# Set one's weight splits shared between GpSimd and VectorE, and set two's first token pieces nine slots later

## The chip, the cores and the metric

The kernel runs on one core of one Trainium2 chip. The metric is the device time of one execution in microseconds (us); lower is better. TensorE multiplies matrices, ScalarE, VectorE and GpSimd do the elementwise work, and SyncE issues the DMA transfers.

## What is computed

The reference, cut to what matters:

```python
def _moe_ref(x, w_gate, w1, w2):            # x: (2304, 512), from a chunked attention
    P = exp(x @ w_gate - max)               # then 8 rounds of row and column scaling
    out = 0
    for e in range(8):
        h = np.maximum(x @ w1[e], 0.0)      # (2304, 1024)
        out += P[:, e:e + 1] * (h @ w2[e])
    return out

def _moe2_ref(x, w_in, w_out):              # d_ff 2048
    h = x @ w_in
    return (h * np.clip(h + 3.0, 0.0, 6.0) / 6.0) @ w_out
```

Everything is float32. The kernel keeps float32 accuracy by splitting every operand into a rounded high part and the remainder (low part), and by doing three matmuls for one.

## The kernel before

After a first stretch (attention, gate, expert 0, up to about 277 us) the 2304 tokens are worked in three sets of 768. In each set the 28 quarter-experts of experts 1 to 7 are 28 **steps**; the loop is `for s in slots`. A step is seven **slots**, and in each slot TensorE does one of seven products of the first layer (a seven-product scheme for 2x2 blocks, six matmuls of 384 columns each, line 937) and, in set one, one of six token tiles of the second layer of the step before (`mm2_chunk`, six matmuls of 512 columns, line 1077). The products of a step share three PSUM banks called `ha`, `hb`, `hc`, drawn from a pool of two: the order of the products is a, b, a, b, c, b, c, and the third bank, c, takes the place of a as soon as a has been read.

What a step needs beside TensorE, in set one:

- VectorE adds the products (`first_sums`, line 979: results called `u2`, `u3`, `p1`) and takes the low part of the first hidden block (`h_out`, line 954). ScalarE copies the first product (line 983), applies the ReLU (958) and rounds to the high part (953, 959); GpSimd subtracts to get the low part of three hidden blocks (960). The next step's `mm2_chunk` reads all of these (`H`).
- The weights of the quarter-expert are prepared once, in set one, and stored for the other sets: seven first-layer blocks in tile `W1` (from raw tile `r1`, with three sums by VectorE, lines 831 and 837), and eight second-layer blocks, four in tile `W2` (from raw tile `r2`) and four in tile `SS` (from `s2`, three sums of `r2` by VectorE, lines 848 and 854). A split is a **piece** (`cut_piece`): ScalarE rounds to the high part (858), then GpSimd or VectorE subtracts for the low part (859). A step has four pieces of `W1` (`w1_piece`, the last one half as wide and on VectorE), two of `W2` (`w2_piece`) and two of `SS` (`w2s_piece`), seven of the eight on GpSimd.
- The stores go through SyncE's queue (`w1_keep` line 875, `w2_store` line 896), as do the loads of raw weights (`raw_load` 808, `raw_load2` 821 to 823). The tile `SS` has a pool of one buffer (line 1556), and so has `s2` (1560); `W2` has two.

The order of the side work is set by a planner: `book` (line 1621) puts an operation into the first slot from `g` on in which the engines' load, by a table of costs, stays under its limits; `book_cuts` (1643) does so for pieces; `at_slot` then files it. Within a slot the work for the products is written first and then the side work, each engine takes its own instructions strictly in the order written, and an instruction that has to wait holds all behind it on its engine. In every fourth step (4, 8, ... 24) VectorE also adds six finished expert sums to the result (line 1085). Conversion of the last layer's weights (`cv_op`, lines 202 to 220) is spread over set one and two.

In set two (28 steps from step 28 on) no weights are split; the tokens of set one's result are cut into pieces for the last layer (`x2_cut`, split by ScalarE 694 and GpSimd 695; `x2_keep`, stored by SyncE 1277), booked by `book_x2` from a fixed slot on (line 1767), followed by the last layer's own weights (`book_ahead`).

Of the kernel before, what the change touches and what calls it, by code (L numbers as in the profile page):

```python
# [9 lines left out]
F32 = mybir.dt.float32  # L10
# [18 lines left out]
def chunk_attention_moe_mlp(  # L29
# [23 lines left out]
    nc = tc.nc  # L53
# [799 lines left out]
        o, x, y, op = ((2, t[:, 1], r[:, 0], ALU.add), (3, r[:, 1], t[:, 2], ALU.subtract))[n - 1]  # L853
        nc.vector.tensor_tensor(out=t[:, o], in0=x, in1=y, op=op)

    def cut_piece(hi, lo, r, lo_eng):

        nc.scalar.activation(out=hi, in_=r, func=AF.Copy)  # L858
        lo_eng.tensor_tensor(out=lo, in0=r, in1=hi.bitcast(F32), op=ALU.subtract)  # L859

    def cut_ops(w, r, o0, o1, lo_eng):

        cut_piece(w[:, o0:o1, 0], w[:, o0:o1, 1], r, lo_eng)

    PIECES = ((0, 2), (2, 4), (4, 6), (6, 7))

    def w1_piece(s, z, lo_eng=nc.gpsimd):
        o0, o1 = PIECES[z]
        r = raw1[s.k].rearrange("p o k f -> p o (k f)")[:, o0 + 1:o1 + 1]
        cut_ops(W1t[s.b].rearrange("p o a k f -> p o a (k f)"), r, o0, o1, lo_eng)  # L870
        if z == 3:
            raw1.pop(s.k)

    def w1_keep(s):
# [4 lines left out]

    W2t = {}  # L880

    def w2_piece(s, z, lo_eng=nc.gpsimd):
        if z == 0:
            W2t[s.i] = pools["W2"].tile([128, 4, 2, 256], F32R, tag="W2", name=f"W2_{s.i}")
        cut_ops(W2t[s.i], raw2[s.k][:, 2 * z:2 * z + 2], 2 * z, 2 * z + 2, lo_eng)

    SS = {}

    def w2s_piece(k, z):
        if z == 0:  # L890
            SS[k] = pools["SS"].tile([128, 4, 2, 256], F32R, tag="SS", name=f"SS_{k}")
        cut_ops(SS[k], raw2[k, "s"][:, 2 * z:2 * z + 2], 2 * z, 2 * z + 2, nc.gpsimd)

    def w2_store(k, o, t):
        n = t.shape[1]
# [448 lines left out]
    with tc.manual_schedule():  # L1344
# [221 lines left out]
        def at_slot(i, z, fn, *a):  # L1566
            sides.setdefault((7 * i + z) // 7, {}).setdefault((7 * i + z) % 7, []).append((fn, *a))
# [53 lines left out]
        def book(g, fn, *a, dve=0.0, act=0.0, pool=0.0):  # L1621
            need = (("DVE", dve), ("ACT", act), ("POOL", pool))
            def full(e, c):
                v = load[e]
                if e != "DVE":
                    if g < 7 * TURN + 7:
                        return v[g] + c > CAP[e]
                    return max(sum(v[g - 2:g + 1]), sum(v[g - 1:g + 2]), sum(v[g:g + 3])) + c > 6.05
                old = new = 0.0
                for i in range(max(0, g - 7), g + 8):  # L1630
                    old = max(0.0, old + v[i] - (2.08 if i >= 7 * TURN else 2.23))
                    new = max(0.0, new + v[i] + c * (i == g) - (2.08 if i >= 7 * TURN else 2.23))
                    if new > max(SLACK, old):
                        return True
                return False

            while any(c and full(e, c) for e, c in need):
                g += 1
            use(g, dve, act, pool)
            at_slot(0, g, fn, *a)  # L1640
            return g

        def book_cuts(g, end, pieces):
            for fn, *a in pieces:
                if a[-1] == 3 and fn is w1_piece:
                    g = book(g + 1, fn, *a, nc.vector, act=0.4, dve=0.8)
                else:
                    g = book(g, fn, *a, act=0.62, pool=1.3)
            assert g < end, (g, end, pieces)
            return g  # L1650

        for s in slots[:NEXP]:
            if s.i > 1:
                g = max(7, 7 * (s.i - 2) + 3)
                for n in range(NSUM):
                    g = book(g, w1_sum, s.k, n, dve=1.0 if n == 0 else 0.8)
            if s.i == 1:
                for z in range(4):
                    at_slot(0, z, w1_piece, s, z, nc.vector if z > 1 else nc.gpsimd)
                at_slot(0, 6, w1_keep, s)  # L1660
            elif s.i:
                g = book_cuts(max(g + 1, 7 * (s.i - 1)), 7 * s.i,
                              [(w1_piece, s, z) for z in range(4)])
                at_slot(0, g + 2, w1_keep, s)
            if s.i and s.i + 2 < NEXP:
                at_slot(s.i - 1, 4, raw_load, s.k + 2)
        for s in slots[:TURN]:
            if s.i:
                at_slot(s.i - 1, 0, raw_load2, s.k)
            g = 7 * s.i  # L1670
            if s.i:
                h = book_cuts(g + 1, g + 7, [(w2_piece, s, z) for z in range(2)])
            else:
                h = g + 3
                at_slot(0, g + 1, w2_piece, s, 0)
                at_slot(0, h, w2_piece, s, 1, nc.vector)
            at_slot(0, h + 2, w2_keep, s)
            for n in range(NSUM):
                g = book(g, w2_sum, s.k, n, dve=1.0 if n == 0 else 0.8)
            h = book_cuts(max(g, h) + 1, 7 * s.i + 8,  # L1680
                          [(w2s_piece, s.k, z) for z in range(2)])
            at_slot(0, h + 2, w2s_keep, s.k)

        for s in slots[NEXP:]:
            if s.load:
# [78 lines left out]

        at_slot(ends[0], 6, x2_T, 0, 0)
        at_slot(ends[0], 6, x2_T, 0, 1)
        g = 7 * ends[0] + 9
        for kl in range(2):
            g = book_x2(g, 0, kl, 3)
        g = book_ahead(g + 4, range(NEXP, NEXP + NG4))  # L1770
# [107 lines left out]
```

## Time and profile before

| | us |
|---|---|
| median of 3 runs | 1917.66 (1917.62 to 1919.47) |
| profiled execution | 1915.93 |
| its span, first to last instruction | 1914.2 |
| TensorE busy in the span | 1892.2 (99%) |
| VectorE busy | 1587.4 (83%) |
| GpSimd busy | 1240.1 (65%) |
| ScalarE busy | 813.9 (43%) |

The profiled execution is 1.7 us under the median. TensorE's idle time in the whole span is 22 us, so what the side engines do counts only where TensorE waits for them. Set one's steps run from about 277 us to 731 us.

### The profile page before, as it was taken

The page shows a single profiled execution, that of the slowest core. Times are in us where ns is not written, and L with a number is a line of the kernel's source. Part 1 is how long each engine was busy: PE and PEld are TensorE (multiplying, and loading weights), DVE is VectorE, ACT ScalarE, POOL GpSimd, SP SyncE. Part 2 cuts the span into 40 slices and gives each one's busy share as a digit, 9 for nine tenths or more (in the row PEclk, how much of TensorE's full clock was granted, in tenths as well). Part 3 has the DMA queues.
Part 4 walks back from the last instruction along what each step waited for, and adds up shares of the span by engine and source line. Part 5 has one row for each costly group of instructions (what it writes and reads, how often), then busy time and mean ns, then how long its engine had stood idle before and what let it go on. Part 6 is the DMA issues. An engine that isn't in the chain of part 4 may idle for free.

```text
span 1914.2 us, 34452 instructions
## 1 busy us (share of the span) xinstructions
PE 1892.2 (99%) x11915; PEld 1810.9 (95%) x11915; DVE 1587.4 (83%) x2366; ACT 813.9 (43%) x1632; POOL 1240.1 (65%) x1072
## 2 busy tenths in 40 slices
PE   9999999999999999999999999999999999999998
PEld 8789998988889898999999999999999999999998
DVE  6677577788788858999999989898888888797867
ACT  5333335555555543434343333233333345454452
POOL 3323248888888875768887556576788755566544
PEclk9999999999999999999999999999999999999999
DMA  9987569999999997999999899989999999999984
GB/s 212 225 221 232 207 222 355 329 314 320 316 324 315 326 345 269 365 339 352 359 375 395 292 331 328 314 295 343 343 363 372 387 343 335 339 304 310 291 266 147
DMA packets 353661, 594.18 MB, mean 310 GB/s; under 512 B 56512, under 2 KB 171600, under 8 KB 353360
## 3 DMA queue, kind: packets, MB, share of 16 engines
q1 hardware_dynamic: 353488, 591.98, 90.0%
q8 instruction: 95, 1.56, 0.3%
q14 instruction: 78, 0.64, 0.1%
HBM read 405.68 MB, written 186.20 MB: 309 GB/s over the span
## 4 chain that ended last, share of the span: by engine, by line
PE 85%; DVE 8%; DMA 3%; issue 2%; ACT 1%; POOL 0%; DVEq 0%; SPq 0%; ACTq 0%; POOLq 0%
PE o L1195 18%; PE hb L937 16%; PE ha L937 10%; PE acc L1077 10%; PE hc L937 10%; PE o L1185 9%; PE h L587 5%; PE acc L624 5%; DVE u L979 1%; DMA W2R<-wsc 1%; PE pv_None L439 1%; DVE accM L1220 1%; PE sc_None L351 1%; DVE r L837 1%; DMA wsc<-W 1%
## 5 line engine op out<-in xcount | busy, mean ns | idle before, releaser
L937 PE MATMUL hb<-X,W 128*128 128x384 f32 x1944 | 393.2, 337 | 5.4 <-DVE u L979 5.1
L937 PEld LDWEIGHTS hb<-X,W 128*128 128x128 f32 x1944 | 338.8, 188 | 17.5 <-DVE u L979 11.0
L1195 PE MATMUL o<-Hb,W2R 128*128 128x384 f32 x1296 | 275.5, 334 | 1.8 <-DMA W2R<-wsc 1.3
L937 PE MATMUL hc<-X,W 128*128 128x384 f32 x1296 | 261.1, 336 | 1.5 <-DVE H L954 0.7
L937 PE MATMUL ha<-X,W 128*128 128x384 f32 x1296 | 260.7, 335 | 0.6 <-DVE m L1257 0.6
L1077 PE MATMUL acc<-W,H 128*128 128x512 f32 x1008 | 258.9, 391 | 0.7 <-POOL H L960 0.5
L937 PEld LDWEIGHTS hc<-X,W 128*128 128x128 f32 x1296 | 226.3, 188 | 8.2 <-DVE u L979 2.5
L1195 PEld LDWEIGHTS o<-Hb,W2R 128*128 128x128 f32 x1296 | 229.1, 188 | 2.4 <-issue 1.6
L1220 DVE SCALAR_TENSOR_TENSOR accM<-o,accM 128x768 f32<-128x768 f32 x209 | 198.6, 950 | 39.1 <-PE o L1195 25.0
L937 PEld LDWEIGHTS ha<-X,W 128*128 128x128 f32 x1296 | 226.0, 188 | 3.8 <-DVE m L1257 0.9
L1195 PE MATMUL o<-Ha,W2R 128*128 128x384 f32 x1056 | 227.3, 334 | 1.4 <-ACT accM L1218 1.4
L859 POOL TENSOR_TENSOR Hb<-u,Hb 128x384 fp32r<-128x384 f32 x144 | 164.7, 1146 | 80.2 <-ACT Hb L858 69.7
L1077 PEld LDWEIGHTS acc<-W,H 128*128 128x128 f32 x1008 | 187.4, 188 | 30.2 <-POOL H L960 3.2
L859 POOL TENSOR_TENSOR W<-r,W 128x512 fp32r<-128x512 f32 (+1 forms) x139 | 193.9, 1426 | 15.4 <-ACT W L858 15.2
L1195 PEld LDWEIGHTS o<-Ha,W2R 128*128 128x128 f32 x1056 | 186.8, 188 | 2.0 <-ACT accM L1218 1.7
L859 POOL TENSOR_TENSOR Ha<-t,Ha 128x384 fp32r<-128x384 f32 x89 | 98.6, 1108 | 90.6 <-ACT Ha L858 81.0
L859 POOL TENSOR_TENSOR Hb<-p,Hb 128x384 fp32r<-128x384 f32 x94 | 111.5, 1186 | 66.1 <-ACT Hb L858 45.4
L979 DVE TENSOR_TENSOR u<-hc,u 128x384 f32<-128x384 f32 x216 | 118.4, 548 | 41.2 <-PE hc L937 41.1
L979 DVE TENSOR_TENSOR u<-hb,p 128x384 f32<-128x384 f32 x216 | 118.5, 549 | 32.6 <-PE hb L937 27.0
L859 POOL TENSOR_TENSOR Ha<-u,Ha 128x384 fp32r<-128x384 f32 x96 | 112.5, 1173 | 48.1 <-ACT Ha L858 43.0
L858 ACT ACTIVATE Hb<-u 128x384 fp32r<-128x384 f32 x144 | 75.6, 525 | 157.0 <-DVE u L675 54.2
L1185 PE MATMUL o<-W2R,Hb 128*128 128x256 f32 x837 | 129.0, 281 | 0.0
(201 smaller groups left out, 3587.2 us busy)
## 6 DMA issues: line engine op xcount, KB each, us to landing
W2R<-wsc SPq DMA_DIRECT2D x280, 512.0 KB, 6.0
W<-wsc SPq DMA_DIRECT2D x504, 256.0 KB, 5.8
wsc<-W SPq DMA_DIRECT2D x28, 1792.0 KB, 7.3
wsc<-SS SPq DMA_DIRECT2D x28, 1024.0 KB, 9.1
wsc<-m SPq DMA_DIRECT2D x112, 256.0 KB, 5.9
r<-in_moe_w_dram SPq DMA_DIRECT2D x84, 256.0 KB, 7.9
wsc<-W SPq DMA_DIRECT2D x28, 768.0 KB, 8.5
X<-xsc SPq DMA_DIRECT2D x21, 768.0 KB, 8.1
```

The lines of the kernel that those rows point to most:

```text
L351: nc.tensor.matmul(out=sc[z][64 * par:64 * par + 64, g * CH:(g + 1) * CH], lhsT=qT[64 * z:64 * z + 64, 2 * hp + par, c * CH:(c + 1) * CH], ...
L439: nc.tensor.matmul(out=ps[c][64 * par:64 * par + 64, g * CH:(g + 1) * CH], lhsT=vt[tt][64 * c:64 * c + 64, 2 * hp + par, :], rhs=aT[64 * c ...
L587: nc.tensor.matmul(out=hps[:, :n], lhsT=w[:, a, kk, :], rhs=xx[:, kk, :], start=(kk == 0 and a == 0 and xx is xh), stop=(kk == KD - 1 and ...
L624: nc.tensor.matmul(out=o, lhsT=w[:, a, c] if turned else hx[:, c], rhs=hx[:, :n] if turned else w[:, a, :], start=(f == 0 and hx is hi and ...
L858: nc.scalar.activation(out=hi, in_=r, func=AF.Copy)
L859: lo_eng.tensor_tensor(out=lo, in0=r, in1=hi.bitcast(F32), op=ALU.subtract)
L937: nc.tensor.matmul(out=ps[:, :HN], lhsT=W1t[s.b][:, wo, a, kl, :], rhs=x[:, b, kl, :], start=(start and kl == 0 and a == 0 and b == 0), st ...
L979: nc.vector.tensor_tensor(out=o, in0=ps[b][:, :HN], in1=x, op=ALU.add)
L1077: nc.tensor.matmul(out=o, lhsT=s.Hs[:, fi, hx, t * 128:(t + 1) * 128], rhs=w[:, 0::3, a, :] if fi == 0 else w[:, 1:3, a, :], start=(s.j % ...
L1185: nc.tensor.matmul(out=o[:, t * 256:(t + 1) * 256], lhsT=hs[q][:, b, t * 128:(t + 1) * 128], rhs=w[:, q, a, :], start=(q, a, b) == mm[0] a ...
L1195: nc.tensor.matmul(out=ps[:, d, :HN], lhsT=w[:, q, a, d * 128:(d + 1) * 128], rhs=hs[q][:, b, :], start=(q, a, b) == mm[0] and not again, ...
L1220: nc.vector.scalar_tensor_tensor(out=dst, in0=src, scalar=sc, in1=dst, op0=ALU.mult, op1=ALU.add)
```

## The change

In set one the low parts of two more pieces of a step are taken by VectorE: the second piece of `W2` and the first piece of `SS`. A piece can now be made in two halves (`half=0` is ScalarE's rounding, `half=1` the subtraction), and for the three pieces on VectorE the rounding is booked at least one slot ahead of the subtraction. The sums of `s2` are booked around the first piece of `SS`; a variable `kept2` keeps a step's sums and pieces of `SS` behind the last piece of the step before. The planner's costs of the sums go down from 1.0 and 0.8 to 0.9 and 0.7. In the first step the second piece of `W2` goes to GpSimd and two pieces of `W1` are a slot later. In set two the first token piece is booked from slot 18 of the set on, not 9; all that is booked behind it moves too.

The core of the diff (signatures that only pass `half` and `lo_eng` on are left out):

```diff
+    def cut_piece(hi, lo, r, lo_eng, half=None):
+        if half != 1:
+            nc.scalar.activation(out=hi, in_=r, func=AF.Copy)
+        if half != 0:
+            lo_eng.tensor_tensor(out=lo, in0=r, in1=hi.bitcast(F32), op=ALU.subtract)
...
-    def w2s_piece(k, z):
-        if z == 0:
+    def w2s_piece(k, z, lo_eng=nc.gpsimd, half=None):
+        if half != 1 and k not in SS:
             SS[k] = pools["SS"].tile([128, 4, 2, 256], F32R, tag="SS", name=f"SS_{k}")
...
+        ON_DVE = {w1_piece: 3, w2_piece: 1, w2s_piece: 0}
         def book_cuts(g, end, pieces):
             for fn, *a in pieces:
-                if a[-1] == 3 and fn is w1_piece:
-                    g = book(g + 1, fn, *a, nc.vector, act=0.4, dve=0.8)
+                if a[-1] == ON_DVE[fn]:
+                    w = 0.4 if fn is w1_piece else 0.62
+                    g = book(g + 1, fn, *a, nc.vector, 0, act=w)
+                    g = book(g + 1, fn, *a, nc.vector, 1, dve=w + 0.25)
...
-                    at_slot(0, z, w1_piece, s, z, nc.vector if z > 1 else nc.gpsimd)
+                    at_slot(0, z + z // 2, w1_piece, s, z, nc.vector if z > 1 else nc.gpsimd)
...
-                at_slot(0, h, w2_piece, s, 1, nc.vector)
+                at_slot(0, h, w2_piece, s, 1)
             at_slot(0, h + 2, w2_keep, s)
-            for n in range(NSUM):
-                g = book(g, w2_sum, s.k, n, dve=1.0 if n == 0 else 0.8)
-            h = book_cuts(max(g, h) + 1, 7 * s.i + 8,
-                          [(w2s_piece, s.k, z) for z in range(2)])
+            g = max(g, kept2)
+            g = book(g, w2_sum, s.k, 0, dve=0.9)
+            c = book(g + 1, w2s_piece, s.k, 0, nc.vector, 0, act=0.62)
+            g = book(g + 1, w2_sum, s.k, 1, dve=0.7)
+            c = book(max(c, g) + 1, w2s_piece, s.k, 0, nc.vector, 1, dve=0.87)
+            g = book(g, w2_sum, s.k, 2, dve=0.7)
+            h = book_cuts(g + 1, 7 * s.i + 12, [(w2s_piece, s.k, 1)])
+            h = max(c, h)
             at_slot(0, h + 2, w2s_keep, s.k)
+            kept2 = h + 1
...
-        g = 7 * ends[0] + 9
+        g = 7 * ends[0] + 18
```

What this makes of the instruction order is shown at three places. In the rows below a name's first number is the step (of `W1`: the buffer; of `r1`, the quarter-expert), and the brackets name what the instruction waits for (`DMAHW` is a lane of DMA transfers; `Activation` is ScalarE, `Pool` GpSimd).

**ScalarE in step 5**, the step behind an expert's end, from the rounding of `H_5` on. Before:

```order
L953 ACTIVATE H_5_4470<-ha_5_4463 128x384 [waits PE_49,Pool_49]
L858 ACTIVATE W1_0_3126<-r1_6_4281 128x256
L858 ACTIVATE W2_5_4507<-r2_5_4338 128x2x256 [waits DMAHW3_49,DMAHW2_49]
L858 ACTIVATE SS_5_4547<-s2_5_4477 128x2x256 [waits DMAHW0_49,DVE_49]
L858 ACTIVATE SS_5_4547<-s2_5_4477 128x2x256 [waits DVE_49]
L958 ACTIVATE u3_5_4542<-u3_5_4542 128x384 [waits DVE_49]
L959 ACTIVATE H_5_4470<-u3_5_4542 128x384 [waits Activation_49]
```

Now:

```order
L859 ACTIVATE SS_4_4361<-s2_4_4334 128x2x256 [waits DVE_49]
L955 ACTIVATE H_5_4466<-ha_5_4459 128x384 [waits PE_49,Pool_49]
L859 ACTIVATE W1_0_3126<-r1_6_4278 128x256
L859 ACTIVATE W2_5_4518<-r2_5_4336 128x2x256 [waits DMAHW1_49,DMAHW0_49]
L859 ACTIVATE W2_5_4518<-r2_5_4336 128x2x256 [waits DMAHW3_49,DMAHW2_49]
L859 ACTIVATE SS_5_4543<-s2_5_4521 128x2x256 [waits DMAHW5_49,DVE_49]
L960 ACTIVATE u3_5_4536<-u3_5_4536 128x384 [waits DVE_49]
L961 ACTIVATE H_5_4466<-u3_5_4536 128x384 [waits Activation_49]
```

The second piece of `SS_4`, which stood in step 4, is now rounded in step 5, and `SS_5`, in the same single buffer, is begun in that step too.

**SyncE at the end of step 4 and in step 5**, around the store of `SS_4`. Before:

```order
L896 DMA wsc2_2_100<-W2_4_4360 128x3x512 [waits DMAHW7_49,Pool_49]
L896 DMA wsc2_2_100<-SS_4_4399 128x4x512 [waits DMAHW0_49,Pool_49]
L821 DMA r2_6_4481<-in_moe_w2_dram 128x2x256 [waits DMAHW1_49]
L822 DMA r2_6_4481<-in_moe_w2_dram 128x256 [waits DMAHW2_49]
L823 DMA r2_6_4481<-in_moe_w2_dram 128x256 [waits DMAHW3_49]
```

Now:

```order
L898 DMA wsc2_2_100<-W2_4_4358 128x3x512 [waits DMAHW7_49,DVE_49,Pool_49]
L821 DMA r2_6_4474<-in_moe_w2_dram 128x2x256 [waits DMAHW0_49,DVE_49]
L822 DMA r2_6_4474<-in_moe_w2_dram 128x256 [waits DMAHW1_49]
L823 DMA r2_6_4474<-in_moe_w2_dram 128x256 [waits DMAHW2_49]
L184 DMA cv_8_4478<-in_moe2_w_out_dram 128x1024 [waits DMAHW3_49]
L184 DMA cv_9_4480<-in_moe2_w_out_dram 128x1024 [waits DMAHW4_49]
L898 DMA wsc2_2_100<-SS_4_4361 128x4x512 [waits DMAHW5_49,Pool_49]
```

The store of `SS_4` has moved behind the loads of step 5 (its slot was the sixth of step 4 and is now the fourth of step 5); the first rounding of `SS_5` waits for it on lane 5. The same holds at steps 9, 13, 17, 21 and 25.

**VectorE in step 0**, the last four sums but one of the step. Before:

```order
L979 TENSOR_TENSOR u3_0_3836<-hb_0_3806,p1_0_3794 128x384 [waits PE_49]
L859 TENSOR_TENSOR W1_1_3784<-r1_1_3130,W1_1_3784 128x256 [waits Activation_49]
L859 TENSOR_TENSOR W2_0_3817<-r2_0_3517,W2_0_3817 128x2x256 [waits DMAHW0_49,Activation_49]
L979 TENSOR_TENSOR u3_0_3836<-hc_0_3842,u3_0_3836 128x384 [waits DVE_49,PE_49]
L557 TENSOR_REDUCE scs_3861<-cp7_3859 128x8 [waits PE_49]
```

Now:

```order
L981 TENSOR_TENSOR u3_0_3839<-hb_0_3804,p1_0_3794 128x384 [waits PE_49]
L861 TENSOR_TENSOR W1_1_3784<-r1_1_3130,W1_1_3784 128x2x256 [waits Activation_49]
L981 TENSOR_TENSOR u3_0_3839<-hc_0_3845,u3_0_3839 128x384 [waits DVE_49,PE_49]
L861 TENSOR_TENSOR W1_1_3784<-r1_1_3130,W1_1_3784 128x256 [waits Activation_49]
L557 TENSOR_REDUCE scs_3864<-cp7_3862 128x8 [waits PE_49]
```

The narrow piece of `W1` now stands behind the sum of `u3`, and its rounding on ScalarE stands behind that sum's ReLU and rounding; behind it on VectorE are four small operations of the gate's scaling and the sum `p1`.

## Rows read from the trace of the kernel before

**Rows 1.** The page, busy time of each engine in the span.

```profile
PE 1892.2 (99%) x11915; PEld 1810.9 (95%) x11915; DVE 1587.4 (83%) x2366; ACT 813.9 (43%) x1632; POOL 1240.1 (65%) x1072
```

**Rows 2.** Stretches: length, busy PE, PEld, DVE, ACT, POOL, granted clock, DMA share, GB/s.

```profile
280.00:300.00 20.00, 17.82 (x91) 15.83 (x90) 17.55 (x24) 9.63 (x21) 16.39 (x13) 1.00 0.83 290
300.00:320.00 20.00, 18.59 (x90) 15.92 (x89) 12.38 (x17) 11.12 (x22) 17.21 (x14) 1.00 1.06 385
...
310.00:725.00 415.00, 411.81 (x2048) 369.23 (x2047) 325.65 (x417) 217.96 (x435) 336.26 (x257) 1.00 0.93 324
...
1910.00:1914.20 4.20, 0.00 (x0) 0.00 (x0) 0.83 (x2) 0.00 (x0) 0.00 (x0) 0.80 0.50 170
```

**Rows 3.** Waits (us in total, times, longest): PE's in the span, ACT's in 310:725.

```profile
PE hb L937 <- DVE u L979: 5.1, 10, 1.6
...
ACT SS L858 <- DMA wsc<-SS: 9.8, 6, 4.4
```

**Rows 4.** The tile SS in 310:725, durations in ns min/median/max, and its store's landing.

```profile
L858 ACT ACTIVATE SS<-s x52: 612/621/635, 315.8 to 709.9; 128x512 fp32r<-128x512 f32 x52
L859 POOL TENSOR_TENSOR SS<-s,SS x52: 1277/1476/1765, 316.5 to 711.3; 128x512 fp32r<-128x512 f32 x52
...
DMA to landing us min/median/max: 6.6/9.1/12.7
```

**Rows 5.** Groups of instructions in 310:725: busy us, mean ns of one, idle before.

```profile
L831 DVE TENSOR_TENSOR r<-r 128x512 f32<-128x512 f32 x24 | 29.7, 1239 | 0.0
L859 DVE TENSOR_TENSOR W<-r,W 128x256 fp32r<-128x256 f32 x25 | 28.9, 1157 | 0.0
...
L859 POOL TENSOR_TENSOR W<-r,W 128x512 fp32r<-128x512 f32 x126 | 176.0, 1429 | 0.7 <-ACT W L858 0.5
```

**Rows 6.** Timeline of PE in the step that starts at 415.16: start us, us.

```profile
415.16 1.30 PE L937 MATMUL ha<-X,W 128*128 128x384 f32 x6
416.30 1.54 PE L1077 MATMUL acc<-W,H 128*128 128x512 f32 x6
417.69 1.21 PE L937 MATMUL hb<-X,W 128*128 128x384 f32 x6
...
424.94 1.22 PE L937 MATMUL hc<-X,W 128*128 128x384 f32 x6
...
430.84 1.21 PE L937 MATMUL ha<-X,W 128*128 128x384 f32 x6
```

**Rows 7.** Timelines of ACT and POOL in that step.

```profile
428.89 0.53 ACT L958 ACTIVATE u<-u 128x384 f32<-128x384 f32 x1 [5.12 <-DVE u L979]
...
418.82 7.86 POOL L859 TENSOR_TENSOR W<-r,W 128x512 fp32r<-128x512 f32 x5
...
431.02 1.03 POOL L960 TENSOR_TENSOR H<-p,H 128x384 fp32r<-128x384 f32 x1
```

**Rows 8.** Timelines of PE, DVE, ACT and POOL at set one's start.

```profile
283.95 1.31 PE L937 MATMUL hb<-X,W 128*128 128x384 f32 x6 [1.57 <-DVE u L979]
...
277.56 0.68 DVE L848 TENSOR_TENSOR s<-r 128x512 f32<-128x512 f32 x1
278.28 0.43 DVE L854 TENSOR_TENSOR s<-s,r 128x256 f32<-128x256 f32 x1
...
286.22 0.55 DVE L979 TENSOR_TENSOR p<-hb,p 128x384 f32<-128x384 f32 x1
...
285.33 0.53 ACT L958 ACTIVATE u<-u 128x384 f32<-128x384 f32 x1 [2.52 <-DVE u L979]
...
279.10 3.79 POOL L859 TENSOR_TENSOR W<-r,W 128x512 fp32r<-128x512 f32 x3 [12.79 <-ACT W L858]
```

**Rows 9.** Timelines of PE and ACT at set two's start.

```profile
744.67 0.61 PE L1195 MATMUL o<-Hb,W2R 128*128 128x384 f32 x2 [0.56 <-POOL Hb L859]
...
754.42 0.79 PE L1195 MATMUL o<-Ha,W2R 128*128 128x384 f32 x3 [1.37 <-ACT accM L1218]
...
753.15 0.52 ACT L694 ACTIVATE m<-m 128x384 fp32r<-128x384 f32 x1 [2.26 <-DMA x2sc<-m]
```

More of the change, by code (lines that the diff above doesn't have):

```diff
@@ L854, in w2_sum, with cut_ops, w1_piece @@
         nc.vector.tensor_tensor(out=t[:, o], in0=x, in1=y, op=op)
[L856 to L863, printed above, removed]
+    def cut_piece(hi, lo, r, lo_eng, half=None):
[3 more added lines that the diff above has]
+            lo_eng.tensor_tensor(out=lo, in0=r, in1=hi.bitcast(F32), op=ALU.subtract)
+    def cut_ops(w, r, o0, o1, lo_eng, half=None):
+        cut_piece(w[:, o0:o1, 0], w[:, o0:o1, 1], r, lo_eng, half)
     PIECES = ((0, 2), (2, 4), (4, 6), (6, 7))
-    def w1_piece(s, z, lo_eng=nc.gpsimd):
+    def w1_piece(s, z, lo_eng=nc.gpsimd, half=None):
         o0, o1 = PIECES[z]
         r = raw1[s.k].rearrange("p o k f -> p o (k f)")[:, o0 + 1:o1 + 1]
-        cut_ops(W1t[s.b].rearrange("p o a k f -> p o a (k f)"), r, o0, o1, lo_eng)
-        if z == 3:
+        cut_ops(W1t[s.b].rearrange("p o a k f -> p o a (k f)"), r, o0, o1, lo_eng, half)
+        if z == 3 and half != 0:
             raw1.pop(s.k)
@@ L880, in chunk_attention_moe_mlp, with w2_piece @@
     W2t = {}
-    def w2_piece(s, z, lo_eng=nc.gpsimd):
+    def w2_piece(s, z, lo_eng=nc.gpsimd, half=None):
         if z == 0:
             W2t[s.i] = pools["W2"].tile([128, 4, 2, 256], F32R, tag="W2", name=f"W2_{s.i}")
-        cut_ops(W2t[s.i], raw2[s.k][:, 2 * z:2 * z + 2], 2 * z, 2 * z + 2, lo_eng)
+        cut_ops(W2t[s.i], raw2[s.k][:, 2 * z:2 * z + 2], 2 * z, 2 * z + 2, lo_eng, half)
     SS = {}
-    def w2s_piece(k, z):
-        if z == 0:
+    def w2s_piece(k, z, lo_eng=nc.gpsimd, half=None):
+        if half != 1 and k not in SS:
             SS[k] = pools["SS"].tile([128, 4, 2, 256], F32R, tag="SS", name=f"SS_{k}")
-        cut_ops(SS[k], raw2[k, "s"][:, 2 * z:2 * z + 2], 2 * z, 2 * z + 2, nc.gpsimd)
+        cut_ops(SS[k], raw2[k, "s"][:, 2 * z:2 * z + 2], 2 * z, 2 * z + 2, lo_eng, half)
     def w2_store(k, o, t):
@@ L1655, in chunk_attention_moe_mlp @@
                 for n in range(NSUM):
-                    g = book(g, w1_sum, s.k, n, dve=1.0 if n == 0 else 0.8)
+                    g = book(g, w1_sum, s.k, n, dve=0.9 if n == 0 else 0.7)
             if s.i == 1:
                 for z in range(4):
-                    at_slot(0, z, w1_piece, s, z, nc.vector if z > 1 else nc.gpsimd)
+                    at_slot(0, z + z // 2, w1_piece, s, z, nc.vector if z > 1 else nc.gpsimd)
                 at_slot(0, 6, w1_keep, s)
@@ L1666, in chunk_attention_moe_mlp @@
                 at_slot(s.i - 1, 4, raw_load, s.k + 2)
+        kept2 = 0
         for s in slots[:TURN]:
```

## Prediction

> **What bounds the kernel now.** I read the page's busy times first. TensorE is busy 1892.2 of 1914.2 us [rows 1], so only its 22 us of idle time can be won, and side work costs only where TensorE comes to wait for it. Next, the table of stretches: in set one's steady part (310 to 725 us) TensorE is busy 411.81 of 415.00 us, idle for 3.2; in the first 40 us of the set it loses 2.18 and 1.41, together 3.6 [rows 2]. Last, the waits by pair: the ten waits of the second product for VectorE's `u` come to 5.1 us [rows 3]. One of them, 1.57 us, stands at set one's start [rows 8]; at set two's start there are waits of 0.56 and 1.37 us [rows 9]. So what this change touches holds 3.2 + 3.6 + 1.9 = 8.7 us to win at most.
>
> What else those rows show decides the forecast: in the steady part ScalarE already waits six times for the store of the one-buffer tile `SS` (9.8 us, longest 4.4 [rows 3]). TensorE does not feel it, since what stands behind that wait is not due yet.
>
> **The two subtractions.** GpSimd loses 1.43 us (`W2`, [rows 5]) and 1.48 us (`SS`, [rows 4]) a step, 2.9 us. What VectorE gains is bounded by 512-column operations with two SBUF inputs: 0.68 us where GpSimd is idle [rows 8], 1.24 us on average beside it [rows 5], and 1.43 if the operation lasts as long as GpSimd's. I take the middle: about 1 us each. With 256 columns it is alike: 0.43 alone [rows 8], 1.157 in the steady part [rows 5]. VectorE was busy 325.65 of 415 us [rows 2]; 26 steps by 1.4 to 2.9 us add 35 to 75, which still fits. GpSimd is finished some 3 us earlier in a step, so that VectorE's other sums meet it less often, and the steady waits of 3.2 us should mostly go. I put **−3** (0 to −3.2). The stores of `W1` and `W2` go out about a slot later; both tiles have a spare buffer, so that costs nothing. Without it the price would be the wait worked out next, which is just what the tile without one pays.
>
> **The single buffer of SS.** In the steps 5, 9, 13, 17, 21 and 25, behind the ends of experts, the order on ScalarE now holds the second rounding of `SS` for the step before, and then the first rounding for this step, which needs the buffer back, so the store's landing. The store is filed in the same slot as that rounding. Behind the rounding, in ScalarE's strict order, stand the ReLU and rounding of `u3`, `p1` and `u2`, which the next step's second layer reads. I time this from a step's start, by the step at 415.16 us:
>
> - GpSimd's first cut starts at 418.82 − 415.16 = 3.66 [rows 6, 7]. Four cuts end at the last piece of `SS`; with little of VectorE beside them they take 3.79 / 3 = 1.26 us each [rows 8], five in the row of this step 7.86 [rows 7]; at 1.3 each the store goes out at 3.66 + 5.2, about 9.0.
> - With a landing time L the buffer is free at R = 9.0 + L. The stores of `SS` land in 6.6 to 12.7 us, median 9.1 [rows 4]. I take **L = 7.5**, nearer to the short end, because the store follows fewer bytes in these steps (1.3 MB of loads before it) than it did. R = 16.5.
> - ScalarE then rounds `SS` (0.62 [rows 4]), and does the two pairs for `u3` and `p1` (four at 0.53 [rows 7]); GpSimd takes the low part of `p1` in 1.03 [rows 7]: R + 3.8 = 20.3.
> - TensorE starts the next step at 430.84 − 415.16 = 15.68, its first chunk 1.14 later, and the chunk's six matmuls come at (417.69 − 416.30) / 6 = 0.23 us each [rows 6]. The sixth, which needs `p1`'s low part, would start at 15.68 + 1.14 + 5 × 0.23 = 17.97. **First wait: 20.3 − 17.97 = 2.3 us.**
> - VectorE's low part of `SS` stands behind the same rounding, and the sum of `u2` behind that: 0.62 + 0.68 + 0.43 + 0.55 [rows 4, 8], R + 2.3. ScalarE's pair for `u2` ends at R + 3.4, GpSimd's part of it (behind `p1`'s) at R + 4.8; then comes the second cut of `SS`, to R + 6.1, and its store at R + 6.3, landing at R + 6.3 + L = R + 13.8. The following step's first `SS` rounding waits for it, and the rounding of that step's first hidden block stands behind: 0.62 + 0.53, and VectorE's low part 0.55, R + 15.5. TensorE needs the bank that this frees for its fifth product; it does its sixth chunk matmul until R + 4.05, and from there the fifth product is 424.94 − 417.69 = 7.25 us away [rows 6], R + 11.3. **Second wait: 4.2 us.**
>
> The pieces of a later step stand as in a standard step, and a landing fits there again. So 2.3 + 4.15 = 6.45 us, six times: **+38.7**. The same working with L = 6.6 gives (1.4 + 3.25) × 6 = 28, with 9.1 (3.9 + 5.75) × 6 = 58. The first wait is gone at L = 5.2 and the second, which without the first is 2L − 8.46, at L = 4.2.
>
> One rule speaks against the size. The Trainium skill, "DMA: Bandwidth & Descriptors", section "Anatomy of one DMA — SWDGE (gpsimd) path", fits a transfer's time as 2.0 us plus its bytes at 436 GB/s, which for the 1 MB of `SS` makes an estimate of 4.4 us. No store of `SS` in this trace landed under 6.6 us [rows 4], with the DMA engines 93% busy [rows 2], so the trace does not agree. By the page's figure the second wait alone would be left, 0.3 us, and the time would be about 1918, the rival below in which the stores land in time.
>
> **The start of set one.** Now the first step's narrow `W1` piece stands behind the sum of `u3` on VectorE, and its rounding behind the ReLU and rounding of that sum on ScalarE (2 × 0.53 [rows 8]); with its subtraction (0.43 to 1.16 [rows 5, 8]) and four small gate operations (taken at 0.25 each, about half of the 0.43 of a 256-column one) ahead of the sum `p1` (0.55 [rows 8]), the product that takes `p1`'s bank comes about 2.9 us later. The 1.57 us of [rows 8] shrinks less than that costs. I put **+2.7**, with bounds of +1.7 (the subtraction alone on its engines) and +4 (beside GpSimd).
>
> **The start of set two.** The waits of 0.56 and 1.37 us come beside the token pieces, whose rounding on ScalarE waits 2.26 us for a buffer [rows 9]. Pieces that are nine slots later leave that place; they may do the same elsewhere. I put **−1**, between −1.9 and +1.9.
>
> **Sum:** 1915.93 + 38.7 − 3 + 2.7 − 1 = 1953.3 for the profiled execution; the median of the runs is 1.7 above it, so **1955 us**.
>
> **The rivals.**
>
> *The clock falls (1967).* All of the 310 to 725 us stretch ran at a granted 1.00, which is 2.4 GHz, with no wait above 1.6 us; after the last matmul the rows show 0.80 over 4.2 us [rows 2, 3]. If a wait of 4.2 us brings the clock to the lower level, 1.2 GHz, and it stays for as long again, half of that time is lost: 2.1 × 6 = 12.6 on top. The Trainium skill, "TensorE: Matmul & The Clock Gate", section "Why this matters for your kernels", says that idle gaps between bursts of matmuls, if long enough, bring TensorE back to half its rate. No row of this trace has such a gap between matmuls, so nothing here shows it either way.
>
> *VectorE becomes the bound (1940).* If the sums and pieces keep their price beside GpSimd (1.16 and 1.24 [rows 5]) with the two new ones on top, the sum `p1` would be made at 16.45 us of the step where 15.68 is due, 0.77 in each of 27 steps, 21 us; with +2.7 and −1 and no −3 that is 1938.6, and 1.7. Against it: GpSimd ends sooner, so not all of them can meet it. This takes landing times short enough to leave the groups alone.
>
> *The stores land in time (1917).* At L of about 4.2 both waits vanish; with −3, +2.7 and −1 nothing is left that can be told from no change (0.2%, 3.8 us, is about what a measurement of this kernel can tell). Against: 6.6 is the shortest of 26 stores.
>
> *Faster (1909).* GpSimd's shorter work is what ends the waits. Its place is the waits on VectorE in set one, behind sums stretched by GpSimd, and the token pieces of set two; its price all of 3.2 + 3.6 + 1.9, so 1915.9 − 8.7 + 1.7 = 1909. It decides if the landing is at most 4.2 us, or if the planner's slots leave room that I took as used, and the narrow piece at the start is hidden. For it: the ten waits for `u` are of this kind [rows 3]. Against it: the single buffer.
>
> **How the numbers follow.** The forecast has 0.74, the clock 0.06, VectorE 0.05: slower, 0.85 together. In time: 0.06, within 0.2%. Faster: 0.09. The low end, 1925, is L near 5, below any row, where only 1.5 us of the second wait is left (9 us, less the gains); the high end, 1988, is L = 9.1 with the upper bounds (1915.9 + 58 + 4 + 1.9 + 1.7 = 1982) and half of the clock's 12.6. Outside lie the cases of 0.06 and 0.09, and some 0.04 of the others.
>
> **What would show it.** ScalarE's waits for the store of `SS` grow from 9.8 us in six to about 50 in twelve or more, up to 8 or 9 us long. TensorE shows six waits of about 2 us of the second layer for GpSimd's or ScalarE's hidden blocks, and six of about 4 us of the third-bank product for VectorE's low part, in the steps 6 and 7, 10 and 11 and so on, or a step before. Set one is some 38 us longer; at its start one product waits about 2.7 us for VectorE; GpSimd has five cuts in a step and not seven. It is wrong if the stores of `SS` in those steps land within 5 us, or if TensorE's waits stand on VectorE's sums in all steps alike.

## The result and the profile after

| | before | changed |
|---|---|---|
| median of the runs, us | 1918.06 (4 runs) | 1940.38 (4 runs) |
| profiled execution, us | 1915.93 | 1940.99 |
| its span, us | 1914.2 | 1939.2 |

The changed kernel is **slower: 1.0119 times the time of before, 95% interval 1.0101 to 1.0137**, 22 us. The forecast was 1955 us in a range of 1925 to 1988: the sign and the mechanism held, the size was 37 us where 22 came.

The page's busy times of the changed kernel, beside [rows 1]:

```profile
PE 1900.7 (98%) x11915; PEld 1817.5 (94%) x11915; DVE 1576.4 (81%) x2420; ACT 813.9 (42%) x1632; POOL 1158.4 (60%) x1018
```

GpSimd lost 82 us of work, and VectorE, which took it over, did not become busier but 11 us less busy; some of its operations stand further down. So engine load is not where the time went. TensorE's waits (total us, times, longest) and ScalarE's for the store of `SS`, both in 310 to 725 us, show where it did; they answer to [rows 3]:

```profile
PE hc L939 <- DVE H L956: 17.1, 6, 5.4
PE hb L939 <- DVE u L981: 1.9, 2, 1.0
...
ACT SS L859 <- DMA wsc<-SS: 62.4, 11, 8.2
```

Six waits of the third-bank product, 17.1 us, where the kernel before had one of 0.7 in that stretch; and ScalarE's 9.8 us have become 62.4. The six waits, one behind each expert's end (two of them with a shorter wait for `u` ahead), in TensorE's timeline (start, duration, in brackets the idle time before and who ended it):

```profile
379.87 2.29 PE L939 MATMUL hc<-X,W 128*128 128x384 f32 x6 [2.36 <-DVE H L956]
...
449.38 2.29 PE L939 MATMUL hc<-X,W 128*128 128x384 f32 x6 [5.30 <-DVE H L956]
451.47 2.76 PE L1079 MATMUL acc<-W,H 128*128 128x512 f32 x6
454.03 1.46 PE L939 MATMUL hb<-X,W 128*128 128x384 f32 x6
...
512.75 1.34 PE L939 MATMUL hb<-X,W 128*128 128x384 f32 x6 [0.84 <-DVE u L981]
...
516.41 1.33 PE L939 MATMUL hc<-X,W 128*128 128x384 f32 x6 [0.96 <-DVE H L956]
...
577.88 1.32 PE L939 MATMUL hb<-X,W 128*128 128x384 f32 x6 [1.02 <-DVE u L981]
...
581.89 1.31 PE L939 MATMUL hc<-X,W 128*128 128x384 f32 x6 [1.29 <-DVE H L956]
...
650.04 2.29 PE L939 MATMUL hc<-X,W 128*128 128x384 f32 x6 [5.35 <-DVE H L956]
...
717.13 2.09 PE L939 MATMUL hc<-X,W 128*128 128x384 f32 x6 [1.81 <-DVE H L956]
```

The reader should look at the durations too. Six matmuls of 384 columns take 1.21 us and six of 512 columns 1.52 [rows 6]; behind four of these waits the first product takes 2.09 to 2.29 and the chunk after it up to 2.76. That is about half the clock, and the table of stretches says so (its eighth column is the granted clock): behind the wait of 5.30 us, around the two shorter waits near 512 us, and behind the one of 1.81:

```profile
447.00:456.00 9.00, 6.62 (x21) 5.94 (x22) 5.90 (x10) 4.73 (x9) 2.30 (x2) 0.62 0.33 108
512.00:518.00 6.00, 4.29 (x20) 3.66 (x21) 5.24 (x9) 2.35 (x5) 3.55 (x3) 1.00 0.33 128
...
717.30:722.00 4.70, 4.70 (x17) 4.22 (x18) 3.29 (x5) 1.58 (x4) 1.50 (x2) 0.64 0.45 157
```

Adding up what the groups of matmuls behind the four waits took beyond 1.21 and 1.52 gives 8.7 us; TensorE's busy time, 1900.7 us against 1892.2 for the same 11915 matmuls, grew by about as much, 8.5. With the waits, 17.1 + 1.9 + 8.7 = 27.7, less the 3.1 us that the kernel before waited in set one's steady part, 24.6 of the 25.0 us by which the spans differ.

How one such wait comes about, in SyncE's, ScalarE's and VectorE's timelines of the steps 5 and 6:

```profile
359.71 0.38 SPq L898 DMA_DIRECT2D wsc<-SS  x1
...
371.94 0.38 SPq L898 DMA_DIRECT2D wsc<-SS  x1
```

```profile
365.78 0.63 ACT L859 ACTIVATE SS<-s 128x512 fp32r<-128x512 f32 x1 [6.07 <-DMA wsc<-SS]
...
378.22 0.63 ACT L859 ACTIVATE SS<-s 128x512 fp32r<-128x512 f32 x1 [5.91 <-DMA wsc<-SS]
378.75 0.47 ACT L955 ACTIVATE H<-ha 128x384 fp32r<-128x384 f32 x1
```

```profile
379.25 0.56 DVE L956 SCALAR_TENSOR_TENSOR H<-ha,H 128x384 fp32r<-128x384 f32 x1 [2.67 <-ACT H L955]
```

The store of `SS_4` goes out at 359.71, and ScalarE stands until it has landed, at 365.78. Everything behind is late, so that the second piece of `SS_5` is stored at 371.94; the first rounding for `SS_6` waits for that until 378.22, the rounding of `H` comes right behind it and VectorE's low part at 379.25, and the product at 379.87 takes the bank that this has freed. The chain is the second wait of the prediction, instruction by instruction.

### The profile page after: what moved, and what is told of

The parts are those of the page before. It is cut to its first block, busy times and chain, and to the rows that moved or that the text cites. A ratio compares the mean times of both kernels' runs of the same rounds, so it can differ in the third digit from the quotient of the medians.

```text
span 1939.2 us, 34456 instructions
## 1 busy us (share of the span) xinstructions
PE 1900.7 (98%) x11915; PEld 1817.5 (94%) x11915; DVE 1576.4 (81%) x2420; ACT 813.9 (42%) x1632; POOL 1158.4 (60%) x1018
## 4 chain that ended last, share of the span: by engine, by line
PE 78%; DVE 9%; DMA 6%; issue 3%; ACT 2%; POOL 1%; SPq 1%; DVEq 0%; POOLq 0%; ACTq 0%
PE o L1197 16%; PE hb L939 14%; PE hc L939 10%; PE ha L939 9%; PE o L1187 9%; PE acc L1079 8%; PE h L587 5%; PE acc L624 5%; DMA wsc<-SS 3%; DVE u L981 1%; DVE u L1021 1%; DMA wsc<-m 1%; DVE accM L1222 1%; PE sc_None L351 1%; PE pv_None L439 1%
## 5 line engine op out<-in xcount | busy, mean ns | idle before, releaser
L939 PE MATMUL hc<-X,W 128*128 128x384 f32 x1296 | 265.1, 339 | 17.6 <-DVE H L956 17.1
L1222 DVE SCALAR_TENSOR_TENSOR accM<-o,accM 128x768 f32<-128x768 f32 x209 | 198.5, 950 | 42.0 <-PE o L1197 27.7
L861 POOL TENSOR_TENSOR W<-r,W 128x512 fp32r<-128x512 f32 x113 | 160.6, 1448 | 15.5 <-ACT W L859 15.3
L981 DVE TENSOR_TENSOR u<-hc,u 128x384 f32<-128x384 f32 x216 | 118.4, 548 | 33.4 <-PE hc L939 33.1
L962 POOL TENSOR_TENSOR H<-u,H 128x384 fp32r<-128x384 f32 x56 | 58.3, 1042 | 132.8 <-ACT H L961 132.8
```

The costliest lines, as they stand in the source:

```text
L939: nc.tensor.matmul(out=ps[:, :HN], lhsT=W1t[s.b][:, wo, a, kl, :], rhs=x[:, b, kl, :], start=(start and kl == 0 and a == 0 and b == 0), st ...
L962: nc.gpsimd.tensor_tensor(out=lo, in0=src, in1=hf, op=ALU.subtract)
L981: nc.vector.tensor_tensor(out=o, in0=ps[b][:, :HN], in1=x, op=ALU.add)
L1222: nc.vector.scalar_tensor_tensor(out=dst, in0=src, scalar=sc, in1=dst, op0=ALU.mult, op1=ALU.add)
```

## The experiments

Theory A is the prediction's, with the rival on the clock added to it, since the rows above show it: the store of the one-buffer tile holds ScalarE, and the clock falls behind the waits that follow. Theory B is that VectorE cannot carry the two subtractions. Ratios stand against runs of the kernel before on the same chip, with 95% intervals.

**Two half tiles.**

```diff
-        opened("a", "SS", 1, "left")
+        opened("a", "SS", 2, "left")
...
-            SS[k] = pools["SS"].tile([128, 4, 2, 256], F32R, tag="SS", name=f"SS_{k}")
+            SS[k, z] = pools["SS"].tile([128, 2, 2, 256], F32R, tag="SS", name=f"SS_{k}_{z}")
...
+            at_slot(0, c + 2, w2s_keep, s.k, 0)
             h = max(c, h)
-            at_slot(0, h + 2, w2s_keep, s.k)
+            at_slot(0, h + 2, w2s_keep, s.k, 1)
```

> The changed kernel with SS as two tiles of half the size (the same memory, two buffers), each stored when its own piece is done; the order of all roundings and subtractions stays. Theory A (the store of the one-buffer tile holds ScalarE): the six pairs of waits and what the clock loses behind them go, 17.1 us of waits of the third-bank product and 7 to 9 us of matmuls at half clock, so 1940.4 - 25 = about 1915 (1911 to 1919); ScalarE's waits for a store of SS fall from 62 us to under 10. Theory B (the two subtractions on VectorE are too much for it): VectorE does the same work, so 1940, within 3. Theory C (SyncE's queue or the DMA load): two stores instead of one make it no better, 1940 or more.

Measured: 1920.1 us, 1.0014 (1.0005 to 1.0023). Its waits of TensorE in 310 to 725 us, and of ScalarE for the store:

```profile
PE hc L939 <- DVE H L956: 2.2, 3, 1.1
PE hb L939 <- DVE u L981: 1.9, 3, 0.8
...
ACT SS L859 <- DMA wsc<-SS: 23.4, 10, 3.9
```

20 of the 22 us are gone with the order of the roundings and VectorE's work unchanged: B and C fall. The time is 1 us above the expected stretch. The expected "under 10 us" of ScalarE's waits did not come; waits of up to 3.9 us remain, and hardly reach TensorE.

**The order kept, the work back on GpSimd.** Both subtractions are issued where the changed kernel has them, by the other engine.

```diff
+                    eng = nc.vector if fn is w1_piece else nc.gpsimd
...
-                    g = book(g + 1, fn, *a, nc.vector, 1, dve=w + 0.25)
+                    g = book(g + 1, fn, *a, eng, 1, dve=w + 0.25)
...
-            c = book(g + 1, w2s_piece, s.k, 0, nc.vector, 0, act=0.62)
+            c = book(g + 1, w2s_piece, s.k, 0, nc.gpsimd, 0, act=0.62)
...
-            c = book(max(c, g) + 1, w2s_piece, s.k, 0, nc.vector, 1, dve=0.87)
+            c = book(max(c, g) + 1, w2s_piece, s.k, 0, nc.gpsimd, 1, dve=0.87)
```

> The changed kernel with its order kept, but the two subtractions of a step (second piece of W2, first of SS) given back to GpSimd. Theory A (the order of SS's rounding behind the store costs, whichever engine subtracts): still slow, and slower than 1940, since GpSimd's seven cuts put the stores of the six steps 1.3 to 2.9 us later: second wait grows by as much or twice that, 1950 to 1975, taken 1958. Theory B (VectorE is overloaded): back to 1916 to 1920.

Measured: 1949.39 us, 1.0164 (1.0149 to 1.0179); just under the expected stretch. The order costs whichever engine subtracts, and with VectorE's help it is some 9 us less. But the loss is made up otherwise than expected (TensorE in 310 to 748 us):

```profile
PE hc L939 <- DVE H L956: 9.6, 5, 3.8
PE acc L1079 <- POOL W L861: 6.3, 13, 1.5
PE hb L939 <- DVE u L981: 6.0, 6, 2.3
```

The second wait did not grow; instead the second layer waits in thirteen places for `W2`, whose cut GpSimd now ends too late, and the sums of `u` wait more.

**TensorE kept at work in the waits.**

```diff
+        for i, n in ((6, 9), (10, 22), (14, 3), (18, 5), (22, 22), (26, 7)):
+            at_slot(i, 3, fill, i, n)
```

> The changed kernel with extra matmuls of 512 columns ahead of the fifth product of the steps 6, 10, 14, 18, 22 and 26 (9, 22, 3, 5, 22 and 7 of them, at 0.227 us each some 15 us, a little less than the waits there), so that TensorE works where it waited. They add products a second time into a sum, so the output is another one. If the clock falls because TensorE stands still in the wait: the waits are filled, the granted clock stays at 1.00, and the 7 to 9 us of matmuls at half clock go: 1932 (1930 to 1934). If the fall of the clock costs nothing of its own or has another cause: 1940, within 2.

Measured: 1933.66 us, 1.0083 (1.0066 to 1.0100), 6.7 us under the changed kernel. The wait of 5.30 us near 449 is here 22 matmuls and a remainder, and the stretch after it runs at the full clock (TensorE's timeline, and the table of stretches):

```profile
441.38 5.17 PE L1574 MATMUL acc<-W,H 128*128 128x512 f32 x22
446.39 1.52 PE L1079 MATMUL acc<-W,H 128*128 128x512 f32 x6
447.97 1.32 PE L939 MATMUL hc<-X,W 128*128 128x384 f32 x6
449.12 1.52 PE L1079 MATMUL acc<-W,H 128*128 128x512 f32 x6
```

```profile
443.00:452.00 9.00, 8.94 (x43) 7.47 (x42) 5.46 (x9) 3.75 (x8) 1.86 (x2) 1.00 0.22 83
```

At the other five places the granted clock is 1.00 too. 15 us of added work make the kernel faster, because they stand where TensorE stood idle. So the clock's share is about 7 us of the 22 (the two intervals leave some 5 either way; the durations above gave 8.7), and the waits themselves the rest.

**The rounding filed three slots behind the store**, one buffer as before.

```diff
-            c = book(g + 1, w2s_piece, s.k, 0, nc.vector, 0, act=0.62)
+            c = book(max(g + 1, free2), w2s_piece, s.k, 0, nc.vector, 0, act=0.62)
...
+            free2 = h + 2 + 3
```

> The changed kernel with SS's first rounding filed at the earliest three slots (6.7 us) behind the slot of the store that it waits for, and the second piece behind it; one buffer as before, the two subtractions on VectorE. From step 5 on every step then has the pieces in its slots 6 to 8 and the store in slot 10. Theory A: a landing of 4.3 to 6.3 us fits in three slots, the waits go as with two half tiles: 1915 (1911 to 1922); where landings of 8.4 us stay, one or two short waits. Theory B: 1940, within 3.

Measured: 1920.37 us, 1.0013 (1.0003 to 1.0022). ScalarE's waits for the store are 6.9 us in four, and TensorE's 2.6 in 310 to 725 us:

```profile
ACT SS L859 <- DMA wsc<-SS: 6.9, 4, 2.9
```

```profile
PE hb L939 <- DVE u L981: 2.6, 4, 0.7
```

The same buffer and the same engines, another slot, and all but 2 or 3 us of the loss are gone. That makes it the place of the rounding against the store's landing.

**Set two's shift alone**, in the kernel before, and **taken back** in the changed one (`g = 7 * ends[0] + 18` against `+ 9`).

> The kernel before with set two's first token piece at slot 18 of the set and nothing else of the change. The prediction had -1 (-1.9 to +1.9) for it: 1916.5. The traces of the changed kernel and of three of its variants show another account: the waits at set two's start shrink by about 1 us, and new waits for VectorE's u stand between 1000 and 1350 us, 2.6 us in five or six, which before does not have: +1.5, so 1919 (1918 to 1921).

> The changed kernel with set two's first token piece back at slot 9. Set one's six pairs of waits stay. If the shift gains 1 us, 1941; if it costs 1.5 as the traces let think, 1939; either way within 3 of the changed kernel's 1940.4, which shows that set two has no part in the loss.

Measured: 1920.16 us, 1.0009 (1.0000 to 1.0018), and 1941.18 us, 1.0117 (1.0104 to 1.0131), the same as the changed kernel. TensorE's waits from 725 to 1350 us with the shift alone:

```profile
PE hb L937 <- DVE u L979: 3.5, 6, 0.9
PE o L1195 <- DMA W2R<-wsc: 2.6, 3, 1.4
```

The two waits of [rows 9] are indeed gone, 2.0 us; but the waits for `u` grow from 0.6 us in two to 3.5 in six and those for the loads of `W2R` from 1.3 to 2.6. Here the shift moves the waits on and adds a little. It does not do so everywhere: in the same stretch the changed kernel waits 3.9 us with the shift and 5.7 with it taken back.

**Set one's first step as before.**

```diff
-                    at_slot(0, z + z // 2, w1_piece, s, z, nc.vector if z > 1 else nc.gpsimd)
+                    at_slot(0, z, w1_piece, s, z, nc.vector if z > 1 else nc.gpsimd)
...
-                at_slot(0, h, w2_piece, s, 1)
+                at_slot(0, h, w2_piece, s, 1, nc.vector)
```

> The changed kernel with set one's first step as before: the pieces of W1 a slot earlier, the second piece of W2 on VectorE. The prediction had +2.7 for the new order there: it would give 1937.7. The trace shows TensorE losing 5.1 us in the first 50 us of the set, 4.8 before: 1940, within 1.5.

Measured: 1943.81 us, 1.0133 (1.0117 to 1.0148), above the expected 1940 within 1.5 and not faster than the changed kernel. Its start is no better (270 to 320 us):

```profile
PE hb L939 <- DVE u L981: 4.4, 2, 3.6
```

**Two half tiles, each rounding three slots behind its store, set two's shift taken back.** This is both cures together.

> The changed kernel with SS as two tiles of half the size, each piece's rounding filed at the earliest three slots behind the store of its buffer, and set two's first token piece back at slot 9. Theory A (landings that hold ScalarE were all of the loss): no wait for a store of SS longer than 1 us, set one like before or up to 3 us shorter, set two as before: 1914 to 1918, taken 1916.5. Theory B (the two subtractions cost VectorE something of their own): 1919 or more, by waits for its sums in set one above the 2.3 us of before.

Measured: 1930.79 us, 1.0059 (1.0047 to 1.0072): a miss by 14 us. TensorE waits six and twelve times a little, 9.2 us where the kernel before waits 3.1, which is about half of the 12 us lost. VectorE's own waits lead to a cause (310 to 725 us):

```profile
PE hb L939 <- DVE u L981: 5.6, 6, 1.5
PE hc L939 <- DVE H L956: 3.6, 12, 1.5
...
DVE s L848 <- POOL SS L861: 57.2, 22, 3.5
```

`s2`, the tile of the sums, has one buffer as well. Its first sum is written by VectorE when GpSimd has cut the second piece of `SS` for the step before; filed later, that piece holds VectorE, and `u` and the low part of `H` stand behind. In the changed kernel this wait is 24.6 us in twelve, with the rounding three slots late 33.1 in nineteen, and TensorE feels little of it: in the changed kernel the waits of 0.84 and 1.02 us for `u` stand behind it. The expectation had left this second single buffer out. It had also taken ScalarE's waits for a store as at most 1 us; they are 22.8 us in thirteen, the longest 4.9. A second buffer for `s2` was not tried, so this cause is read from the trace alone. Against a load on VectorE speaks that in the next kernels it does the two subtractions in 20 of the 26 steps without loss.

**No piece of SS leaves its step.** In the six steps with the expert sums both subtractions stay on GpSimd and are filed as in the kernel before; in the other steps VectorE has them.

```diff
+            if s.i and s.i % NG4 == 0:
+                for n in range(NSUM):
+                    g = book(g, w2_sum, s.k, n, dve=0.9 if n == 0 else 0.7)
+                h = book_cuts(max(g, h) + 1, 7 * s.i + 12,
+                              [(w2s_piece, s.k, z, nc.gpsimd) for z in range(2)])
+            else:
```

> The changed kernel with one exception: in the steps 4, 8, 12, 16, 20 and 24, in which VectorE also adds six expert sums, both subtractions stay on GpSimd and are filed as in the kernel before; set two's first token piece is back at slot 9. No piece of SS then leaves its step, and each store lies three slots ahead of the next rounding. If a store that holds ScalarE was all that cost, ScalarE waits under 12 us for it, TensorE has no wait above 1.5 us in set one's steady part, and the time is that of before or up to 3 us less: 1914 to 1919, taken 1917. If the two subtractions load VectorE too much in the other steps: 1922 or more, with waits for its sums in all steps.

> The same with set one's first step as before. If the new order of that step costs the 2.7 us of the prediction, 2.7 less than its sister; by the traces (5.1 us lost in the first 50 us of the set against 4.8) the same within 1.

> The same as the first, with set two's first token piece at slot 18. By the run with that shift alone (1.2 us slower, 0 to 3.4): 1 to 2 us more than the first; by the prediction's term 1 less.

Measured: 1917.07 us, 0.9995 (0.9986 to 1.0004); with the old first step 1916.78, 0.9992 (0.9983 to 1.0000); with the shift in set two 1917.24, 0.9996 (0.9987 to 1.0004). TensorE's waits in 310 to 725 us of the first, and ScalarE's for the store:

```profile
PE hc L939 <- DVE H L956: 1.5, 4, 0.5
```

```profile
ACT SS L859 <- DMA wsc<-SS: 27.1, 7, 4.5
```

VectorE carries the two subtractions in 20 of the 26 steps, and TensorE waits 1.5 us where the kernel before waits 3.1. ScalarE still waits 27.1 us for stores, more than expected and more than before; nothing due stands behind those waits. The whole gain left by the change is these 1.6 us, under what can be told from no change. Between the three the first step and the shift make no difference that can be told either. None of them beats the kernel before by more than the measurement tells.

## Why the prediction was right in kind and off in size

- **The single buffer of SS: right in its place, its second wait and its six repetitions; mis-sized by L.** The prediction took 7.5 us for the landing of all twelve stores, worked 6.6 and 9.1 beside it, and set the low end of its range at 5. The first store of a pair landed in 4.3 to 4.6 us in four of the groups and in 6.1 in the first, the second in 5.7 to 8.5 (the waiting rounding's start less the store's issue). The fourth group is left out: there the rounding waited for VectorE's last sum of `s2`; the first of these sums had been held 2.2 us by the late second piece of `SS`:

```profile
ACT SS L859 <- DVE s L854: 6.2, 1, 6.2
```

  The first wait needs L over 5.2, and TensorE has none of it, but for some 0.4 us in the first group: 2.3 x 6 = 14 us of the 38.7 never came. By the prediction's own sign of being wrong (stores that land within 5 us) this wait failed in four groups. The second wait, with two landings in place of one twice, is their sum less 8.46: for the third group 4.4 + 6.0 - 8.46 = 1.9, measured 0.84 + 0.96; for the second 4.35 + 8.5 - 8.46 = 4.4, measured 5.30; for the first 6.1 + 6.3 - 8.46 = 3.9, measured 0.4 + 2.36. Each of the five is within 1.2 us, and together they are 16.4 where 17.0 came. So the working stands, and the landing was the mis-sized term: 25 us forecast for the six, 19.0 measured (17.1 + 1.9).
- **Why the landings were shorter.** The argument pointed the right way (fewer bytes ahead) but stopped at the shortest of the old rows. Its 1.3 MB of loads ahead are 1.6 by the sizes of the transfers (three of `r2`, 512 KB together, and two of `cv` with 512 KB each), and they stand so only in the first group, whose first store took 6.1 us; in the others the two of `cv` are missing. In the table of stretches around a first store, issued at 427.38 and landed at 431.7, the last two numbers of a row are the DMA share and the GB/s:

```profile
427.00:428.50 1.50, 1.50 (x9) 1.27 (x8) 1.12 (x1) 0.00 (x0) 1.50 (x2) 1.00 0.32 120
428.50:431.70 3.20, 3.20 (x18) 2.94 (x18) 3.17 (x7) 0.00 (x0) 0.10 (x1) 1.00 0.95 340
```

  The engines had emptied before it (no transfer between 427.5 and 428.0 us), and then moved 340 x 3.2 = 1.09 MB, little more than the store; from issue to landing it took 4.3 us. The 26 old landings came from fuller queues (93% busy on average, [rows 2]); they were not the price of a store in an empty one. Here the Trainium skill, "DMA: Bandwidth & Descriptors", section "Anatomy of one DMA — SWDGE (gpsimd) path", was closer: its fit, for transfers that GpSimd issues, gives an estimate of 4.4 us for 1 MB, and the rows of the four first stores, which SyncE issues, agree with it (4.3 to 4.6). It does not hold for the second stores, which took up to 8.5 us. The two longest, 8.5 and 8.4 us in the second and the fifth group, have a 512 KB load of `cv` right ahead of them on SyncE; those of 5.7 to 6.3 have none. No run moved that load. The second group's:

```profile
438.04 1.08 SPq L184 DMA_DIRECT2D cv<-in_moe_w_out_dram  x1
439.21 0.45 SPq L898 DMA_DIRECT2D wsc<-SS  x1
```

- **The clock: the rival of 0.06 came, on top of the forecast.** It fell behind four of the six waits, to a granted 0.62 to 0.66, and cost about 7 us by the run that fills the waits, where the rival had 12.6. It fell behind a wait of 1.81 us as well, and did not behind two pairs of about 1 us. The prediction put it with waits of 4.2 us. But the length of the wait does not decide it alone. At set one's start the changed kernel and the one with two half tiles both wait 1.92 us for `u`; the first keeps its clock and the second does not (stretches of the two, in this order):

```profile
285.00:290.00 5.00, 2.97 (x16) 2.38 (x15) 3.44 (x10) 1.79 (x4) 2.27 (x2) 1.00 0.14 41
285.00:290.00 5.00, 4.63 (x17) 4.01 (x15) 3.45 (x9) 1.35 (x3) 2.77 (x3) 0.66 0.05 14
```

  What decides there stays open. The Trainium skill, "TensorE: Matmul & The Clock Gate", section "Why this matters for your kernels", says that idle gaps between bursts of matmuls bring the engine to half its rate. The rows agree that they can, but the clock fell here behind shorter gaps than the page names.
- **The two subtractions: cheaper than taken.** 0.72 and 0.96 us on VectorE in the groups of the changed kernel (busy us, mean ns), where the prediction took 1 each; and VectorE's narrow piece and `W1` sums fell, from 1157 and 1239 ns [rows 5] to 712 and 862, as the argument on meeting GpSimd had it; the sums of `s2` went the other way, the one of 512 columns from 824 to 1422. The rival in which VectorE becomes the bound, whose 16.45 us the prediction does not work out, came to nothing:

```profile
L861 DVE TENSOR_TENSOR SS<-s,SS 128x512 fp32r<-128x512 f32 x26 | 24.9, 959 | 0.8 <-ACT SS L859 0.8
...
L831 DVE TENSOR_TENSOR r<-r 128x512 f32<-128x512 f32 x24 | 20.7, 862 | 0.0
L861 DVE TENSOR_TENSOR W<-r,W 128x512 fp32r<-128x512 f32 x26 | 18.8, 721 | 0.0
L861 DVE TENSOR_TENSOR W<-r,W 128x256 fp32r<-128x256 f32 x25 | 17.8, 712 | 0.0
```

- **The steady waits, -3: in part.** Outside the six groups the changed kernel shows no wait in set one's steady part, so the old 3.1 us are gone there; the kernel without the six groups still waits 1.5. The gain is nearer to 1.6.
- **The start of set one, +2.7: the price was there, the account was not full.** The wait for `p1` came (1.69 us), and that for `u` grew from 1.57 to 1.92, against [rows 8]; the product behind `p1` comes 2.5 us later than before, counted from the set's first product. The table of stretches, and TensorE's timeline:

```profile
280.00:300.00 20.00, 16.05 (x82) 13.98 (x81) 18.27 (x26) 10.84 (x22) 16.53 (x13) 1.00 0.63 206
300.00:320.00 20.00, 19.87 (x98) 17.39 (x97) 13.85 (x21) 9.21 (x19) 11.58 (x10) 1.00 1.05 385
```

```profile
283.96 1.34 PE L939 MATMUL hb<-X,W 128*128 128x384 f32 x6 [1.92 <-DVE u L981]
285.64 1.31 PE L939 MATMUL hc<-X,W 128*128 128x384 f32 x6 [0.34 <-DVE u L981]
...
289.68 1.28 PE L939 MATMUL hb<-X,W 128*128 128x384 f32 x6 [1.69 <-DVE p L981]
```

  In the first 20 us TensorE is busy 16.05 us and was 17.82 [rows 2], 1.8 lost; in the next 19.87 against 18.59, 1.3 back: +0.5. The prediction counted what was added at one place and not the waits further on that no longer come.
- **The start of set two, -1: not there, and its sign is open.** The waits of [rows 9] went, and came again for `u` and for loads of `W2R` up to 1350 us: by the medians of the run of that edit alone +1.3 (0.0 to 3.5 by its interval). With and without the shift the changed kernel takes 1940.4 and 1941.2 us, and the kernel without the six groups 1917.2 and 1917.1.
- **The sum of the errors.** Too much were 14 us for the first wait, 6 for the second and 2 for the start; too little 7 for the clock and 1 for set two: 1955 - 22 + 8 = 1941, measured 1940.4. That the forecast came within 15 us is in part luck: the clock's 7 us, which its sum left out, stand against 20 us too much for the waits.

## What to carry to other kernels

Before work is given to another engine, look at what the new order does to each tile that has one buffer: which instruction waits for its store, what stands behind that instruction on its in-order engine, and when that is due. Price a landing by the queue as it will be at that moment, not by the old landings, and take in that waits on TensorE have a second price, the clock after them. A cure that files work later runs into the next single buffer on the way, so check the chain of tiles to its end.

## What the runs showed that was not expected

- 15 us of added matmuls made the changed kernel 6.7 us faster, since they kept the clock at 1.00 through the waits.
- The clock fell behind a wait of 1.81 us in the steady part, but not behind 0.84 and 0.96 or 1.02 and 1.29 us two chunks apart. At set one's start it stayed at 1.00 behind 1.92 us in the changed kernel and fell behind the same wait in six of its variants (granted 0.66 to 0.68 over 285 to 290 us), such as the one with two half tiles.
- A store of 1 MB landed in 4.3 us where the DMA engines were empty and in 6.6 to 12.7 where they were 93% busy. The second stores of the second and fifth group took 8.4 to 8.5 us and the others 5.7 to 6.3; only those two had a 512 KB load right ahead of them, which no run moved.
- GpSimd 82 us less busy left VectorE, with two more operations a step, 11 us less busy.
